# Eight member lists in half the products, search visits placed later, weight loads queued after row stores

## The chip, the cores and the metric

The kernel runs on one core of a Trainium2 chip. The metric is the device time of one execution in microseconds. Before the change three executions took 1294.56 us (median), 1291.51 and 1298.22 us.

## The reference

Three layers follow one another. The first is a retention layer without softmax: for 8 sequences, 8 heads, 576 positions and head size 64, `ret = (q k^T / 8) * D`, with `D[i, j] = gamma_h ** (i - j)` for `j <= i` and 0 elsewhere, and `out = ret v`. This gives `x` of 4608 rows by 512.

The second is a mixture of 8 experts, each row going to one of them:

```
expert_idx = argmax(x_normalised @ emb_normalised.T / tau)
gate       = softmax(logits)[expert_idx]
out[rows]  = gate * (relu(x[rows] @ w1[e]) @ w2[e])     # w1: 512 x 1024, w2: 1024 x 512
```

The third is a mixture of 8 experts of exactly 576 rows each. All 4608 x 8 logits `x @ w_gate` are walked from the largest to the smallest; a row is given to an expert when the row is still free and the expert has fewer than 576 rows. Then `out[rows] = relu(x[rows] @ w1[e]) @ w2[e]`.

## The kernel before, in words

The program has three stages, and the order of each engine's instructions is written out by hand.

Stage A (to about 205 us) computes retention in 36 tiles of 128 rows, routes each row to an expert of the second layer and scatters it to that expert's part of a buffer in HBM.

Stage B (about 215 to 751 us) runs the second layer's experts, five tiles of 128 rows each. Every fp32 operand is split into a high and a low part, and each product is three matrix multiplications (lines 1247 to 1249 for the first product, line 1321 for the second). For `e = 0` the loop over half columns `n` does all first halves and then all second halves; for later experts the halves `h` alternate. Raw weights come in by SyncE's queue into four `raw` buffers (`w_load`, lines 239 and 241). `w_acc` converts one: ScalarE writes the high part (line 267) and its negative (line 248), and GpSimd issues a DMA that adds the raw weight on top (`w_add`, line 251); a `raw` buffer is free again when that DMA is done. The four conversions for the second weight of `e = 0` (`w_conv` at `n` in `CV = (6, 8, 10, 12)`) use a GpSimd subtraction instead (line 272). Each tile's result `yr` (line 1333, two buffers) is stored to HBM by SyncE (line 1335). SyncE works in the order of the program, so a load that waits for its `raw` buffer holds up what stands behind it. In the gaps VectorE makes the third layer's logits by dot products of `yr` with `wgb`, the gate weights broadcast to all partitions (`pull`, line 1171), and those for a small table `M7` (`mpull`, line 1211); every second `yr` goes through TensorE instead (`ytr`, line 1180).

The third layer's assignment is found by eight searches, one after another, each followed by a member list. A search bisects the threshold of the next expert to fill in seven steps. A step has three visits to TensorE: counts (line 875), a fold (line 888) and a spread (line 950), with VectorE work between; three more visits end the search. The member list (`members`) turns the ranks `rk` of 128 x 40 rows into a list of 576 row numbers: four one-hot tiles `ohb` (line 1083), 40 products of 64 stationary and 20 moving columns in two visits (line 1093), the two sums joined (lines 1058 and 1100), a visit in fp32 that puts the halves at their partitions (line 1104), and `idx` (line 1109). Then GpSimd gathers the rows (line 1379).

Stage C (about 751 to 1296 us) runs the third layer's experts (lines 1399 to 1409 for the transposes and splits, 1454 for the first product, 1487 to 1493 for the second). The searches for the later experts run beside the products of the earlier ones. The class `Issue` plans this order: it holds a planned clock for each engine, threads that yield `(engine, duration)`, and places a thread's next step when the planned clocks reach it. A step on TensorE is planned at the end of the thread's previous step plus `HOP["P"]` = 0.25 us, less the thread's `early`. `early` is 0.7 for the first search and its members and 0.0 for the others.

Of the kernel before, what the change touches and what calls it, by code (L numbers as in the profile page):

```python
# [9 lines left out]
F32 = mybir.dt.float32  # L10
F32R = mybir.dt.float32r
BF = mybir.dt.bfloat16
# [145 lines left out]
def moe_kernel(ctx: ExitStack, tc: tile.TileContext, moe_expert_emb, moe_tau, moe_w1, moe_w2,  # L158
# [88 lines left out]
    def w_neg(hi, lo):  # L247
        A.activation(lo, hi.bitcast(F32), AF.Copy, scale=-1.0)  # L248

    def w_add(hi, lo, after=0.0):  # L250
        G.dma_start(lo, RAW[wpos[1]], accum_op=OP.add)  # L251
        w_done_(hi, lo)
        w_load(after=after)

    def w_acc():
        hi, lo = w_high()
# [418 lines left out]
    def search_tables2():  # L675
        for i, sh in enumerate(SHIFTS):
            V.tensor_scalar(jt[i], j0, sh, None, op0=OP.logical_shift_left)
        kj = sc.tile([128, NJ], I32, name="kj")
        V.tensor_tensor(kj, jt[0], kmin.to_broadcast([128, NJ]), op=OP.bitwise_xor)
        V.tensor_scalar(j27, kj, 31, 1, op0=OP.arith_shift_right, op1=OP.logical_shift_right)  # L680
        V.tensor_tensor(j27, j27, kj, op=OP.bitwise_xor)
        for nm in cst:
            SY.dma_start(cst[nm], c[nm])
        V.tensor_copy(descb, desc)
        V.memset(shf, 0.0)
        V.tensor_copy(shf[:, :64], ident[:64, :64])
        V.tensor_copy(shf[:, 192:], ident[:64, :64])
        V.tensor_tensor(lim.rearrange("p (e t) -> p e t", t=T1), rnk[:, None, :].to_broadcast([128, E, T1]),
                        baseL[:, :, None].to_broadcast([128, E, T1]), op=OP.is_lt)
        V.tensor_scalar(lim, lim, -2.0 * NEG, NEG, op0=OP.mult, op1=OP.add)  # L690
        V.memset(rem, float(CAP2))
        V.memset(frz, 0.0)
# [175 lines left out]
    def tl(name, shape, dt=F32, bufs=1):  # L868
        return sw.tile(list(shape), dt, name=name, bufs=bufs)

    def search(p):
# [149 lines left out]
            V.scalar_tensor_tensor(sn[:, z], sn[:, z], r2[:, z:z + 1], mem[:, z], op0=OP.add, op1=OP.mult)  # L1021
        V.scalar_tensor_tensor(rk, sn[:, 0], 1000.0, sn[:, 1], op0=OP.add, op1=OP.add)
        LST.append(p)
        IS.spawn(members(p, rk), p if p < 2 else 3, IS.t["V"], 0.0 if p else 0.7)
        if p < E - 1:
            yield "V", 1.2
            fo = tl("fo", (128, E))
# [11 lines left out]
            V.tensor_tensor(Lw, Lw, eb(acc), op=OP.min)  # L1039

    LST, MDONE, CHT = [], {}, []
    shf = sw.tile([64, 256], F32, name="shf")
    NQ = 4

    RROK = {}

# [8 lines left out]

    def lcopy(p, ls, lq):
        yield "A", 0.2
        A.activation(ls, lq, AF.Copy)
        RROK[p, 1] = IS.t["A"]

    def members(p, rk):
        if p:
            yield lambda: MDONE.get(p - 1)
        yield "V", 0.6
        rki = tl("rki", (128, NSL), I32)
        V.tensor_copy(rki, rk)
        ai = tl("ai", (128, NSL), I32)
        V.tensor_scalar(ai, rki, 6, None, op0=OP.logical_shift_right)
        V.tensor_scalar(rki, rki, 63, None, op0=OP.bitwise_and)
        yield "V", 0.5  # L1070
        ea = tl("ea", (128, NSL, 2 * T2), BF)
        V.tensor_tensor(ea, eb(ai, 2 * T2),
                        a10.rearrange("p r t -> p (r t)")[:, None, :].to_broadcast([128, NSL, 2 * T2]),
                        op=OP.is_equal)
        ohb = []
        ls = tl("ls", (64, 4 * T2))
        rr = tl("rr", (128, NSL, 2, 2, T2), BF)
        IS.spawn(rrows(p, ea, rr), 1, IS.t["V"])
        for z in range(NQ):
            cz = slice(NSL // NQ * z, NSL // NQ * (z + 1))  # L1080
            yield "V", 0.75
            oq = tl(f"ohb{z}", (128, NSL // NQ, 64), BF)
            V.tensor_tensor(oq, rki[:, cz, None].to_broadcast([128, NSL // NQ, 64]),  # L1083
                            i64[:, None, :].to_broadcast([128, NSL // NQ, 64]), op=OP.is_equal)
            ohb.append(oq)
            if z % 2 == 0:
                continue
            if z == 1:
                yield lambda: RROK.get(p)
            yield "P", 1.2, -1.2 if z < NQ - 1 else 0.0  # L1090
            lq = sr()[:64, :4 * T2]
            for cc in range(NSL // NQ * (z - 1), NSL // NQ * (z + 1)):
                P.matmul(lq, ohb[cc * NQ // NSL][:, cc % (NSL // NQ), :],  # L1093
                         rr[:, cc].rearrange("p r z t -> p (r z t)"),
                         start=(cc % (NSL // 2) == 0), stop=((cc + 1) % (NSL // 2) == 0), skip_group_check=True)
            if z == 1:
                IS.spawn(lcopy(p, ls, lq), 1, IS.t["P"])
        yield lambda: RROK.get((p, 1))
        yield "V", 0.25
        V.tensor_tensor(ls, ls, lq, op=OP.add)  # L1100
        yield "P", 0.4
        lp = sr()
        for r in range(2):
            P.matmul(lp[:, :2 * T2], shf[:, 128 * r:128 * r + 128], ls[:, 2 * T2 * r:2 * T2 * r + 2 * T2], start=(r == 0),  # L1104
                     stop=(r == 1), skip_group_check=True)
        yield "V", 0.2
        idx = sw.tile([128, T2], I32, name="idx", bufs=2)
        with nc.allow_low_precision(reason="sums of two whole numbers below 2**24 are exact"):
            V.tensor_reduce(idx, lp[:, :2 * T2].rearrange("p (z t) -> p t z", z=2), axis=AX.X, op=OP.add)
        MDONE[p] = IS.t["V"]  # L1110
        yield lambda: GATHER[0](p)
        yield "G", 1.25 * T2
        XGAT[p] = [IS.t["G"] - 1.25 * (T2 - 1 - t) + 3.2 for t in range(T2)]
        XG2[p] = GATHER[1](idx)
# [3 lines left out]
    def chain():  # L1118
        for p in range(E):
            yield lambda: 0.0  # L1120
            CHT[0][1] = (0, 3, 2)[min(p, 2)]
            CHT[0][5] = 0.0 if p else 0.7
            yield from search(p)

    with tc.tile_pool(name="mb", bufs=1, reuse_waits="tile") as mb, tc.tile_pool(name="mw", bufs=2, reuse_waits="tile") as mw, \
            tc.tile_pool(name="mps", bufs=1, space=PSUM, reuse_waits="tile") as ps:
        wgb = mb.tile([128, E, DM], F32, name="wgb")
        SY.dma_start(wgb.rearrange("p e d -> p (e d)"), ap(c["w_gate_t"], 0, [[0, 128], [1, DM * E]]))
        wgk = mb.tile([128, KD, E], F32, name="wgk")
        SY.dma_start(wgk, moe2_w_gate.rearrange("(k p) e -> p k e", p=128))  # L1130
        s16 = mb.tile([16, E], F32, name="s16")
# [93 lines left out]
        for e in range(E):  # L1225
# [6 lines left out]
            for n in range(2 * KF):  # L1232
# [21 lines left out]
                if n == 3:  # L1254
                    ylg()
                pull()
                if h and (f % 4 or e == 0):
                    mpull()
                if last and n == 2:
                    lg7 = [ps.tile([128, KD, 128], F32, name="tp", bufs=2).rearrange("p k n -> p (k n)")[:2 * E, :m]  # L1260
# [2 lines left out]
                    next(gg, None)  # L1263
                if e == 0 and h:
                    next(gg, None)
                if e and h and f in (0, 1, 3, 5):
                    w_acc()
                if not e and n in CV:
# [42 lines left out]
            for t in range(T1):  # L1311
                if not last:
                    xtr(e + 1, t)
                    for _ in range((1, 2, 1, 0, 0)[t]):
                        w_acc()
                z = slice(128 * t, 128 * t + 128)
                py = ps.tile([128, DM], F32, name="l2", bufs=2)
                for f in range(KF):
                    wh, wl = w2[f]
                    for n, (a, b) in enumerate(((hh, wh), (hh, wl), (hl, wh))):  # L1320
                        P.matmul(py, a[:, f, z], b, start=(f == 0 and n == 0), stop=(f == KF - 1 and n == 2))  # L1321
                        if last:
                            IS.tick(0.234)
                    if f == 1:
                        ytr()
                    if f == 5:
                        ylg()
                    if f % 2:
                        pull()
                yr = mw.tile([128, ROWY], F32, name="yr", bufs=2)  # L1330
                if last:
                    IS.use("A", 0.7)
                A.activation(yr[:, :DM], py, AF.Copy, scale=gts[e][:, t:t + 1])  # L1333
                V.tensor_copy(yr[:, DM:], xe[:, t, :2])
                SY.dma_start(ybuf[e * CAP1 + 128 * t:e * CAP1 + 128 * t + 128, :], yr)
                if not last:
                    if t % 2 == 0:
                        dots.extend((yr, e * T1 + t, j) for j in range(E))
                    else:
                        ytrq.append((yr, e * T1 + t))  # L1340
                    if t % 2:
                        mpull()
                    if t in (1, 3):
                        mpull()

    with tc.tile_pool(name="oc", bufs=2) as oc:
        with tc.If(tv > 0):  # L1347
# [20 lines left out]
    with tc.tile_pool(name="fb", bufs=1, reuse_waits="tile") as fb, tc.tile_pool(name="fw", bufs=2, reuse_waits="tile") as fw, \  # L1368
# [46 lines left out]
        def conv(p, a, b):  # L1415
            for n in range(a, b):
                yield lambda: RAWAT.get(8 * (E + p) + n) if wpos[1] == 8 * (E + p) + n else None
                yield "A", 1.07
                hl = w_high()
                if p == 0 and n < 4:  # L1420
                    yield "V", 1.23
                    w_low(*hl, V)
                    WAT[p, n] = IS.t["V"]
                    continue
                yield "A", 1.07
                w_neg(*hl)
                yield "G", 1.1
                w_add(*hl, 3.0)
                WAT[p, n] = IS.t["G"] + 3.5

        def evac1(p, f, h, pq):
# [141 lines left out]
```

## Time and profile before

| | us |
|---|---|
| median of three executions | 1294.56 |
| the profiled execution's own time | 1298.07 |
| its span, first to last instruction | 1296.3 |
| TensorE matmul busy | 1217.5 (94%) |
| TensorE weight load busy | 1043.9 (81%) |
| VectorE busy | 713.8 (55%) |
| ScalarE busy | 576.9 (45%) |
| GpSimd busy | 328.8 (25%) |
| mean granted TensorE clock (share of 2.4 GHz) | 0.963 |

Busy time counts the time in which at least one instruction of the engine was under way. Matmuls overlap in the pipeline, so the start of one to the start of the next tells what it costs TensorE, not its listed duration. A wait is put down to the instruction that ended it last.

### The profile page before, as it was taken

How to read it: one execution, taken by the hardware profiler on the slowest of the kernel's cores; microseconds unless marked ns; L12 is line 12 of the kernel's file. 1: busy time of each engine (PE TensorE's matmuls, PEld its weight loads, DVE VectorE, ACT ScalarE, POOL GpSimd, SP SyncE). 2: the span in 40 equal slices, each digit the busy share in tenths (PEclk: the TensorE clock that was granted, in tenths of full speed). 3: DMA queues.
4: the chain of work that ended last, by engine and by line, in shares of the span. 5: the costliest groups of instructions: out<-in, count | busy, mean ns of one | idle time of the engine just before them, and what ended most of it. 6: DMA issues, size and time to landing. Idle time of an engine off the chain costs nothing. (4 is left out here: it accounts for less than half of the span.)

```text
span 1296.3 us, 23772 instructions
## 1 busy us (share of the span) xinstructions
PE 1217.5 (94%) x9031; PEld 1043.9 (81%) x9031; DVE 713.8 (55%) x2330; ACT 576.9 (45%) x1090; POOL 328.8 (25%) x451
## 2 busy tenths in 40 slices
PE   6999976799999999999999969999999999899997
PEld 5888865789898989898887658686868878798896
DVE  4566643866565657576565756575857757021120
ACT  3566643345354535453532044353443535274550
POOL 3253454511121313030100021313133231422211
PEclk8999986899999999999999969999999999899999
DMA  7888854566767768686841244757673756677840
GB/s 261 274 282 283 268 212 147 190 164 177 195 177 183 185 168 206 163 213 159 214 127 42 90 127 119 195 137 189 143 183 85 187 152 155 184 172 182 205 100 37
DMA packets 91742, 224.65 MB, mean 173 GB/s; under 512 B 13671, under 2 KB 14447, under 8 KB 91488
## 3 DMA queue, kind: packets, MB, share of 16 engines
q0 software_dynamic: 28272, 90.35, 32.6%
q1 hardware_dynamic: 63344, 132.67, 30.7%
q8 instruction: 73, 1.20, 0.4%
q14 instruction: 53, 0.43, 0.1%
HBM read 130.26 MB, written 40.28 MB: 132 GB/s over the span
## 5 line engine op out<-in xcount | busy, mean ns | idle before, releaser
L1171 DVE SCALAR_TENSOR_TENSOR jk<-yr,wgb 128x512 bf16<-128x512 f32 x168 | 115.4, 687 | 2.4
L1250 ACT ACTIVATE hh<-l 128x320 fp32r<-128x320 f32 x128 | 55.3, 432 | 124.6 <-PE l L1249 112.3
L1333 ACT ACTIVATE yr<-l,gts 128x512 f32<-128x512 f32 x40 | 27.5, 688 | 168.9 <-PE l L1321 65.5
L251 POOL DMA_DIRECT2D w_0l<-raw x29 | 26.7, 920 | 292.2 <-ACT w_0l L248 261.8
L1436 DVE SCALAR_TENSOR_TENSOR h2l<-l,h2h 128x288 fp32r<-128x288 f32 (+2 forms) x128 | 58.3, 456 | 76.9 <-ACT h2h L1434 76.3
L1251 DVE SCALAR_TENSOR_TENSOR hl<-l,hh 128x320 fp32r<-128x320 f32 x128 | 62.4, 487 | 68.7 <-ACT hh L1250 66.2
L1434 ACT ACTIVATE h2h<-l 128x288 fp32r<-128x288 f32 (+2 forms) x128 | 52.3, 409 | 93.2 <-PE l L1454 92.2
L1461 ACT ACTIVATE o<-l 128x512 f32<-128x512 f32 (+1 forms) x40 | 23.7, 593 | 134.1 <-PE l L1493 83.8
L405 DVE TENSOR_TENSOR sm<-s,dt 128x512 f32<-128x512 f32 (+1 forms) x80 | 48.1, 633 | 57.2 <-PE s L402 44.9
L1468 POOL DMA_INDIRECT out_dram<-o,tid x40 | 42.2, 1056 | 137.9 <-ACT o L1461 90.3
L1379 POOL DMA_INDIRECT xg<-ybuf,idx x40 | 42.8, 1069 | 94.5 <-SPq L1347 58.6
L402 PE MATMUL s<-qT,kT 64*128 64x128 f32 x576 | 45.2, 298 | 11.1 <-DMA qT<-qT 8.6
L717 DVE TENSOR_TENSOR xl<-tp,xh 128x512 fp32r<-128x512 f32 (+1 forms) x41 | 27.6, 676 | 50.7 <-ACT xh L716 36.3
L931 DVE TENSOR_TENSOR cmp<-v,kb 128x1280 bf16<-128x1280 f32 (+1 forms) x42 | 54.4, 1295 | 0.2
L1464 DVE TENSOR_TENSOR o<-o,l 64x512 f32<-64x512 f32 x8 | 5.5, 690 | 86.8 <-ACT o L1461 86.8
L1247 PE MATMUL l<-xh,w_0h 128*128 128x320 f32 x128 | 41.4, 323 | 11.9 <-DVE hl L1251 7.6
L402 PEld LDWEIGHTS s<-qT,kT 64*128 64x128 f32 x576 | 38.0, 198 | 17.1 <-issue 9.4
L251 POOL DMA_DIRECT2D w_3l<-raw x29 | 25.3, 874 | 98.5 <-ACT w_3l L248 70.4
L379 POOL TENSOR_TENSOR kd<-kr,gk 128x512 f32<-128x512 f32 (+1 forms) x32 | 34.5, 1080 | 61.8 <-PE st L438 29.3
L251 POOL DMA_DIRECT2D w_2l<-raw x29 | 24.7, 851 | 97.8 <-ACT w_2l L248 61.7
L534 POOL DMA_INDIRECT xs<-xg,r_sli x36 | 37.0, 1027 | 47.0 <-ACT xg L465 26.3
L423 ACT ACTIVATE xT<-o 128x512 f32<-128x512 f32 x36 | 21.5, 597 | 59.9 <-PE o L420 56.8
(374 smaller groups left out, 4131.2 us busy)
## 6 DMA issues: line engine op xcount, KB each, us to landing
raw<-in_moe_w_dram SPq DMA_DIRECT2D x128, 512.0 KB
w_0l<-raw POOLq DMA_DIRECT2D x29, 512.0 KB
w_1l<-raw POOLq DMA_DIRECT2D x29, 512.0 KB
w_2l<-raw POOLq DMA_DIRECT2D x29, 512.0 KB
w_3l<-raw POOLq DMA_DIRECT2D x29, 512.0 KB
ybuf<-yr SPq DMA_DIRECT2D x40, 257.0 KB
xt<-xs SPq DMA_DIRECT2D x39, 261.0 KB
kT<-kT SPq DMA_DIRECT2D x36, 256.0 KB
```

The costliest lines, as they stand in the source:

```text
L251: G.dma_start(lo, RAW[wpos[1]], accum_op=OP.add)
L402: P.matmul(sp[e][:, hp, :], kT[r, hp, :], qT[r, hp, :], start=True, stop=True, skip_group_check=True)
L405: V.tensor_tensor(sm[z, e, :, z], sp[e][z, :, z], dt_t[z, e, :, z], op=OP.mult)
L931: V.tensor_tensor(cmp, bc(v, ALLC, nj), kb.bitcast(F32)[:, None, :].to_broadcast([128, NSL, nj]), op=OP.is_ge)
L1171: V.scalar_tensor_tensor(jk, yr[:, :DM], 1.0, wgb[:, j, :], op0=OP.mult, op1=OP.mult, accum_out=L2V[:, cc, j:j + 1])
L1247: P.matmul(pp, wh[:, fz], xh[:, kk, z], start=(kk == 0), stop=False)
L1250: A.activation(hh[:, f, z], pp, AF.Relu)
L1251: V.scalar_tensor_tensor(hl[:, f, z], pp, 0.0, hh.bitcast(F32)[:, f, z], op0=OP.max, op1=OP.subtract)
L1379: G.indirect_dma_start(out=xg[:m, t, :], out_offset=None, in_=ybuf, in_offset=bass.IndirectOffsetOnAxis(ap=idx[:m, t:t + 1], axis=0))
L1434: A.activation(h2h[:, f, z], pq, AF.Relu)
L1436: V.scalar_tensor_tensor(h2l[:, f, z], pq, 0.0, h2h.bitcast(F32)[:, f, z], op0=OP.max, op1=OP.subtract)
L1468: st = G.indirect_dma_start(out=out, out_offset=bass.IndirectOffsetOnAxis(ap=TID[p][:m, t:t + 1], axis=0), in_=o[:m], in_offset=None)
```

## The change

`early` becomes `LAZY` = -0.35 for the searches and members from the third on, so that their TensorE steps are planned 0.6 us after the operand's planned end. The member list multiplies two 128-row chunks at once: 20 products of 128 stationary and 40 moving columns in one visit, of whose four blocks the two on the diagonal are used; ScalarE copies one and VectorE the other into a bf16 tile `ls` of 128 partitions, and the last visit is in bf16 with `shf` on 128 partitions. In stage B the load that followed each conversion moves: for `e > 0` to every even `n` of the first product, and to the end of each tile of the second, behind the row store. In stage C it stays where it was. The load of `wgb` moves from the start of stage B to `n == 6` of `e = 0`, and the table's dot products in `e = 0` begin at `n = 12` instead of `n = 8`.

```diff
-    def w_add(hi, lo, after=0.0):
+    def w_add(hi, lo):
         G.dma_start(lo, RAW[wpos[1]], accum_op=OP.add)
         w_done_(hi, lo)
-        w_load(after=after)
...
-        V.tensor_copy(shf[:, :64], ident[:64, :64])
-        V.tensor_copy(shf[:, 192:], ident[:64, :64])
+        for z in HALVES:
+            V.tensor_copy(shf[z, :64], ident[z, z])
+            V.tensor_copy(shf[z, 192:], ident[z, z])
...
-        IS.spawn(members(p, rk), p if p < 2 else 3, IS.t["V"], 0.0 if p else 0.7)
+        IS.spawn(members(p, rk), p if p < 2 else 3, IS.t["V"], (0.7, 0.0, LAZY)[min(p, 2)])
...
-    shf = sw.tile([64, 256], F32, name="shf")
-    NQ = 4
+    shf = sw.tile([128, 256], BF, name="shf")
+    NQ, LAZY = 4, -0.35
...
-        A.activation(ls, lq, AF.Copy)
+        A.activation(ls[:64], lq[:64, :4 * T2], AF.Copy)
...
-            if z % 2 == 0:
-                continue
-            if z == 1:
-                yield lambda: RROK.get(p)
-            yield "P", 1.2, -1.2 if z < NQ - 1 else 0.0
-            lq = sr()[:64, :4 * T2]
-            for cc in range(NSL // NQ * (z - 1), NSL // NQ * (z + 1)):
-                P.matmul(lq, ohb[cc * NQ // NSL][:, cc % (NSL // NQ), :],
-                         rr[:, cc].rearrange("p r z t -> p (r z t)"),
-                         start=(cc % (NSL // 2) == 0), stop=((cc + 1) % (NSL // 2) == 0), skip_group_check=True)
-            if z == 1:
-                IS.spawn(lcopy(p, ls, lq), 1, IS.t["P"])
+        yield lambda: RROK.get(p)
+        yield "P", 0.6
+        lq = sr()[:, :8 * T2]
+        for cc in range(0, NSL, 2):
+            c0 = cc % (NSL // NQ)
+            P.matmul(lq, ohb[cc * NQ // NSL][:, c0:c0 + 2, :].rearrange("p c j -> p (c j)"),
+                     rr[:, cc:cc + 2].rearrange("p c r z t -> p (c r z t)"),
+                     start=(cc == 0), stop=(cc == NSL - 2), skip_group_check=True)
+        IS.spawn(lcopy(p, ls, lq), 1, IS.t["P"])
+        yield "V", 0.2
+        V.tensor_copy(ls[64:], lq[64:, 4 * T2:])
         yield lambda: RROK.get((p, 1))
-        yield "V", 0.25
-        V.tensor_tensor(ls, ls, lq, op=OP.add)
...
-            CHT[0][5] = 0.0 if p else 0.7
+            CHT[0][5] = (0.7, 0.0, LAZY)[min(p, 2)]
...
-        SY.dma_start(wgb.rearrange("p e d -> p (e d)"), ap(c["w_gate_t"], 0, [[0, 128], [1, DM * E]]))
...
-                if h and (f % 4 or e == 0):
+                if e == 0 and n == 6:
+                    SY.dma_start(wgb.rearrange("p e d -> p (e d)"), ap(c["w_gate_t"], 0, [[0, 128], [1, DM * E]]))
+                if h and (f % 4 if e else f > 3):
                     mpull()
...
+                if e and not h:
+                    w_load()
                 if e and h and f in (0, 1, 3, 5):
                     w_acc()
...
                     if t in (1, 3):
                         mpull()
+                    w_load()
...
-                w_add(*hl, 3.0)
+                w_add(*hl)
+                w_load(after=3.0)
```

## Rows read from the trace of the kernel before

**Rows 1.** Windows (from:to, length; busy PE, PEld, DVE, ACT, POOL; PEclk, DMA, GB/s).
```profile
771.00:1129.40 358.40, 345.59 (x2532) 280.36 (x2532) 220.04 (x724) 150.21 (x286) 101.72 (x124) 0.97 0.62 158
1129.40:1183.30 53.90, 53.90 (x325) 47.99 (x324) 11.11 (x22) 28.86 (x55) 12.17 (x18) 1.00 0.73 178
```
**Rows 2.** Timeline of PE round two product visits of a member list (start, duration, instruction).
```profile
1103.37 0.40 PE L1493 MATMUL l<-w_2h,h2l 128*128 128x512 f32 x1
1103.70 0.80 PE L1093 MATMUL srb<-rr,ohb 128*64 128x20 bf16 x20
...
1104.77 0.40 PE L1493 MATMUL l<-w_2l,h2h 128*128 128x512 f32 x1
```
**Rows 3.** Timeline of PE round the last visit of a member list.
```profile
1096.94 0.49 PE L1493 MATMUL l<-w_2h,h2l 128*128 128x512 f32 x1
1097.37 0.61 PE L1104 MATMUL srb<-ls,shf 64*128 64x10 f32 x4
...
1098.24 0.40 PE L1493 MATMUL l<-w_2l,h2h 128*128 128x512 f32 x1
```
**Rows 4.** Timeline of PE round a counts visit of a search.
```profile
1054.74 0.39 PE L1489 MATMUL l<-w_1l,h2h 128*64 128x512 f32 x1
1054.97 0.41 PE L875 MATMUL srb<-oh,cmp 128*128 128x32 bf16 x10
...
1055.55 0.39 PE L1489 MATMUL l<-w_2l,h2h 128*64 128x512 f32 x1
```
**Rows 5.** Timeline of PE round the first member list, end of stage B.
```profile
737.50 0.40 PE L1321 MATMUL l<-w_1h,hh 128*128 128x512 f32 x1
...
741.45 0.80 PE L1321 MATMUL l<-w_1h,hl 128*128 128x512 f32 x1
```
**Rows 6.** Windows of 10 us in which the granted clock fell (columns as in rows 1).
```profile
250.00:260.00 10.00, 9.44 (x46) 9.22 (x47) 9.52 (x45) 2.23 (x5) 5.85 (x11) 0.70 0.34 106
740.00:750.00 10.00, 7.63 (x31) 5.35 (x30) 4.82 (x18) 1.63 (x2) 0.00 (x0) 0.66 0.06 23
1040.00:1050.00 10.00, 10.00 (x57) 7.05 (x55) 4.58 (x14) 0.60 (x1) 6.20 (x6) 0.83 0.79 238
1110.00:1120.00 10.00, 9.45 (x31) 7.71 (x32) 0.34 (x2) 0.60 (x1) 4.39 (x7) 0.69 0.74 216
```
**Rows 7.** Waits of PE, 809 to 1130 us (us in total, times, longest).
```profile
PE srb L1104 <- DVE ls L1100: 3.5, 1, 3.5
...
PE srb L875 <- DVE cmp L931: 1.6, 3, 0.9
PE srb L888 <- DVE cs L884: 1.3, 3, 0.6
```
**Rows 8.** Timeline: last split of the third expert's rows, its first product.
```profile
898.38 1.01 DVE L1409 TENSOR_TENSOR xl<-tp,xh 128x512 fp32r<-128x512 f32 x2
...
910.99 0.30 PE L1454 MATMUL l<-xh,w_0h 128*128 128x288 f32 x1
```
**Rows 9.** Waits of PE, 255 to 672 us (stage B from its second expert).
```profile
PE tp L1180 <- ACT yr L1333: 3.6, 6, 1.2
```
**Rows 10.** Timeline of ACT in stage B: a third tile's result.
```profile
341.25 0.69 ACT L1333 ACTIVATE yr<-l,gts 128x512 f32<-128x512 f32 x1 [5.80 <-DMA ybuf<-yr]
```
**Rows 11.** Timeline of SyncE's queue just before it.
```profile
334.96 5.12 SPq L239 DMA_DIRECT2D raw<-in_moe_w_dram  x2
```
**Rows 12.** Waits of PE, 205 to 262 us (the first expert of stage B).
```profile
PE l L1247 <- DVE hl L1251: 5.8, 2, 4.3
```
**Rows 13.** Timeline of DVE, first expert of stage B: a stretched dot product, a late eviction.
```profile
239.44 2.50 DVE L1211 SCALAR_TENSOR_TENSOR jk<-wz,wgb 128x512 bf16<-128x512 f32 x1
...
244.90 2.44 DVE L196 SCALAR_TENSOR_TENSOR g_l<-g_kf,g_l 128x40 f32<-128x40 f32 x1
...
250.02 0.48 DVE L1251 SCALAR_TENSOR_TENSOR hl<-l,hh 128x320 fp32r<-128x320 f32 x1
```
**Rows 14.** Timeline of POOL beside it.
```profile
238.98 2.41 POOL L272 TENSOR_TENSOR w_1l<-raw,w_1h 128x1024 fp32r<-128x1024 f32 x1 [0.27 <-ACT w_1h L267]
```

More of the change, by code (lines that the diff above doesn't have):

```diff
@@ L1075, in members @@
         ohb = []
-        ls = tl("ls", (64, 4 * T2))
+        ls = tl("ls", (128, 4 * T2), BF)
         rr = tl("rr", (128, NSL, 2, 2, T2), BF)
```

## The prediction

> **What bounds the kernel now.** I read the windows by stage first, then TensorE's waits in each stage, then the timeline where a wait or a visit of the search stands. The reader is to see that TensorE sets the end nearly everywhere, and that what can be won is the time in which it does something other than expert products, waits, or runs at its lower clock. The 358.4 us from 771 to 1129 hold the rest of expert 0 and experts 1 to 4 of stage C with the searches beside them; expert 5 alone, with no search, takes 53.9 us [rows 1]. Five such experts would take 270, so the searches cost nearly 90 us in that stretch, all of it on TensorE's path: VectorE is busy 220 us of the 358 and is not the bound. Most of a search's visits do not wait. They cost the switch and their own products, so I price visits by the start of a product before to the start of one after.
>
> **The member list's visits, the largest term.** From 1103.37 to 1104.77 two expert products and one visit of 20 small products pass [rows 2]. The two alone take 2 x 0.234 = 0.47 (the planner's figure for 512 columns, which the undisturbed stretch bears out), so a visit costs 0.93 us, and there are two per list. The last visit costs 1098.24 - 1096.94 - 0.47 = 0.83 [rows 3]. A list thus costs 2 x 0.93 + 0.83 = 2.69. The new visit has 20 products with 128 stationary columns. The nearest row is a counts visit: ten products of 128 by 32 in bf16 cost 0.81 - 0.47 = 0.34 [rows 4], of which the first 0.07 or so is the switch, so ten more cost 0.27 and twenty 0.61; 40 moving columns in place of 32 add about 0.04 to 0.07. I take 0.65. Bounds: 0.61, and 0.93, as an old visit with the same count. The new last visit has two bf16 products where the old one had four fp32 passes: between nothing and the 0.34 of ten products; I take 0.20, the side of few products. A list falls from 2.69 to 0.85, a gain of 1.84 (1.42 to 2.08). Seven lists lie in the stretch from 771 to 1129: 12.9 us (9.9 to 14.6). VectorE and ScalarE have the same number of steps per list as before (an add becomes a copy) and gain or lose nothing.
>
> The first list stands at the end of stage B, where TensorE goes from 737.50 to 741.45 with two products between [rows 5]: 3.95 - 0.47 = 3.48. This one is still planned early (0.7), so a wait for the last one-hot tile and one for the copies stay, about 0.9 together; with 0.85 of work the visit costs 1.75, a gain of 1.7 (0 to 2.6). The list itself isn't late: the gather starts only after the branch at line 1347, when all of stage B is stored. In the window 740 to 750 the granted clock is 0.66 [rows 6], so (1 - 0.66) x 10 = 3.4 us of it are lost to the lower of the two levels, 1.2 GHz, right after this thin stretch. With the thin stretch halved I count half of that: 1.7 (0 to 3.4).
>
> **Slack from the third search on.** From 809 us TensorE waits 1.6 us for a comparison and 1.3 for a fold's operand, and some smaller ones [rows 7]. Placed 0.35 later, two thirds of these should go: 2.0 of 2.9 (0 to 2.9). The window 1040 to 1050 has a clock of 0.83 with TensorE busy all the time [rows 6], 1.7 us lost; there are two such windows, the other at 980 to 990, both right behind two list visits and a fold in close order. With half the list work there I take 2.0 of 3.4 (0 to 3.4).
>
> The longest wait is 3.5 us at 1107, for VectorE's add of the last list [rows 7]; behind it the clock is 0.69 in 1110 to 1120, another 3.1 [rows 6]. The add no longer exists, but what held VectorE I do not see, and a copy may be held the same way: 3.0 of 6.6 (0 to 6.6). This may be an event of the profiled execution, whose 1298.07 lies 3.5 above the median.
>
> The slack's price: a search has 24 TensorE steps, so it ends 24 x 0.35 = 8.4 us later, its list 0.7 more, and this adds up from the third search on. Who waits is the expert whose rows are gathered late. Its tightest place is the third expert: its last split ends at 899.39, its first product starts at 910.99 [rows 8], 11.6 us of room, of which the shift takes 9.1 and TensorE's own gain until then about 5. I charge 1.5 us (-8 to 0). Later experts have more room: the last list has its products at 1103 to 1106 [rows 2], and its expert starts two experts of 53.9 us after 1129.4 [rows 1], at 1237; the 131 us between are more than six delays of 9.1.
>
> **Loads behind row stores.** From the second expert of stage B on, TensorE waits six times, 3.6 us in all, for a result `yr` that ScalarE wrote late [rows 9]. ScalarE waited 5.80 for the row store to free the buffer [rows 10], and the store stood in SyncE's queue behind raw loads that waited for their own buffer, two of them over 5.12 us [rows 11]. After the change the store is issued first. Loads leave up to one tile later (about 6 us), but four buffers are ahead and by the loops each is converted some 20 us or more after it is loaded. The `xt` load also moves ahead of one raw load; the `wz` loads stay behind one. I take 3.4 of 3.6 (-2 to 3.6).
>
> **The start of stage B.** In the first expert TensorE waits 5.8 us in two pieces for `hl` evictions [rows 12]; then 250 to 260 has a clock of 0.70, 3.0 us lost [rows 6]. VectorE is late because single instructions on it are stretched to the end of a GpSimd subtraction: a dot product takes 2.50 us beside GpSimd's 238.98 to 241.39, and a gate step on 40 elements 2.44 beside the next one, and so the eviction comes at 250.02 [rows 13, 14]. Without the four dot products of `n` = 8 to 11, I lay VectorE's list out again: at 239.44 a gate step is stretched instead, the eviction of `n = 9` comes 0.6 earlier, the step that started at 244.90 starts near 243.7, before GpSimd's third subtraction, and the eviction of `n = 10` comes near 245. The third and fourth subtractions then stretch later gate steps, and waits of about 2.8 in smaller pieces stay. Gain 3.0 and 1.3 of the clock: 4.3 (-3 to 8.8). The lower bound is for `wgb`, which now leaves SyncE near 235 in place of 217 and meets other loads: if it lands after about 249, VectorE's first dot product holds back the evictions behind it. The dot products left out here fill gaps of VectorE in the seventh expert.
>
> A rule of the Trainium skill speaks against this term (SBUF — State Buffer, "SBUF: two separate sides"): VectorE and GpSimd share one pair of ports as an exclusive lock, and a VectorE operation with two SBUF inputs, or in a two-port mode, blocks for the whole of a GpSimd operation that reads SBUF. Rows 13 and 14 agree: 2.50 and 2.44 us for instructions that end with GpSimd's. By that rule the lock outlives the dot products, since the gate's steps have SBUF inputs too, and if each subtraction still costs one eviction its whole length, the sum lacks 4.3.
>
> **The sum.** 12.9 + 1.7 + 1.7 + 2.0 + 2.0 + 3.0 - 1.5 + 3.4 + 4.3 = 29.5. The profiled execution took 1298.07 (its span 1296.3 and 1.8 around it), which gives 1268.6. From the median, without the 3.0 for the late add, it is 1294.56 - 26.5 = 1268.1. I predict 1268.5.
>
> **The rivals.**
> Only the products shrink: the visits' waits and the clock's falls stay, or move to other visits, because TensorE reaches a visit earlier than planned (a visit of 0.34 is planned with 0.5). For it: the planner's figures are larger than the rows. Against it: 0.35 of slack is more than most of the waits. The gain is then 12.9 + 1.7 and the stores' 3.4, together 18.0: 1280 from the profiled execution, 1277 from the median; I say 1278.
>
> The lock stays: GpSimd's four subtractions each stretch a gate step and hold an eviction. For it: three gate steps were stretched already. Against it: between them VectorE has 3 us less to do. The start's 4.3 go: 1273.
>
> Nothing to be measured: the first term goes into the place where TensorE waits for gathered rows, because what ends the wait (search, list, gather) is no faster. For it: the gather of an expert can only start when its list is done. Against it: the third expert has 11.6 us of room [rows 8], and later experts have more. The time is within 6 of 1294.56.
>
> Slower: the delayed searches reach the experts. For a loss, experts 2 to 6 would each have to wait for their rows. The price is the delay itself, 9.1 us for each of the five: 45.5, less 29.5, so 1298 + 16 = 1314. It decides where the delay, 9.1 us for the third expert, exceeds its room of 11.6 plus what is still early; only the third is near that.
>
> **How the numbers follow.** Forecast 0.48 (1261 to 1276 alone), only the products 0.18, the lock 0.17, nothing 0.10, slower 0.07. The first three are all faster by over 0.5% (6.5 us, below 1288.1; about what a measurement of this kernel can tell from none): 0.83. Within: 0.10. Slower: 0.07. The range takes in the first three with their bounds: below, all terms near their better end, 1255; above, the lists at 9.9 with the stores alone, 1286.
>
> **What would show it.** Right: 20 products at line 1093's successor in one visit, about 0.65 between neighbours, and four fewer passes in the last visit; the interval between the first products of experts 1 to 5 shorter by near 2 us each; no wait for `yr` in stage B; SyncE's stores at once behind `yr`; an `hl` wait of under 3 us near 245; windows at 740 and 1040 at the full clock. Wrong: a list visit above 0.93; TensorE waiting for the third expert's rows; ScalarE waiting for raw weights in stage B; VectorE waiting for `wgb`.

## The result and the profile after

The changed kernel takes 1274.75 us (median of 4 runs, 1272.62 to 1278.59), the kernel before 1295.41 beside it (4 runs, 1291.51 to 1298.22): ratio 0.9853 [0.9832, 0.9874], faster by 1.5%. The prediction was 1268.5 with a range of 1255 to 1286. The profiled execution of the changed kernel took 1273.87, its span 1272.1, so the spans differ by 24.2 us where the sum had 29.5.

The page of the changed kernel, its head, TensorE's share and the clock in 40 slices:
```profile
span 1272.1 us, 23381 instructions
PE 1197.8 (94%) x8855; PEld 1026.9 (81%) x8855; DVE 716.4 (56%) x2332; ACT 578.7 (45%) x1090; POOL 326.3 (26%) x451
...
PEclk9999986999999999999999979998989999999999
```
TensorE is still the bound at 94%, with 176 instructions fewer: a list had 40 small products and 4 passes and has 20 and 2, and there are eight lists (8 x 22).

Timeline of TensorE round the two visits of one list in the changed kernel (they answer to [rows 2, 3]):
```profile
797.22 0.40 PE L1495 MATMUL l<-w_0h,h2l 128*128 128x512 f32 x1
797.45 0.68 PE L1091 MATMUL srb<-rr,ohb 128*128 128x40 bf16 x20
797.98 0.47 PE L1495 MATMUL l<-w_1h,h2h 128*128 128x512 f32 x1
798.29 0.40 PE L1495 MATMUL l<-w_1l,h2h 128*128 128x512 f32 x1
...
800.39 0.39 PE L1495 MATMUL l<-w_2l,h2h 128*128 128x512 f32 x1
800.62 0.20 PE L1101 MATMUL srb<-ls,shf 128*128 128x10 bf16 x2
800.69 0.47 PE L1495 MATMUL l<-w_2h,h2l 128*128 128x512 f32 x1
801.00 0.39 PE L1495 MATMUL l<-w_3h,h2h 128*128 128x512 f32 x1
```
The product right behind a visit is stretched too (0.31 us to the next start in place of 0.23), so I count as in [rows 2, 3], from the product before a visit to the second product after it, less the two products' 0.47. The product visit costs 798.29 - 797.22 - 0.47 = 0.60 and the last visit 801.00 - 800.39 - 0.47 = 0.14: 0.74 a list where I had 0.85 and the kernel before 2.69.

Windows of the changed kernel: stage C from the first product of expert 0 to that of expert 7, the same less its first 5 us and last two experts, and four stretches of 10 us (from:to, length; busy PE, PEld, DVE, ACT, POOL; PEclk, DMA, GB/s):
```profile
746.40:1213.20 466.80, 450.65 (x3068) 372.53 (x3068) 250.35 (x789) 212.43 (x400) 125.03 (x160) 0.96 0.64 164
751.50:1099.50 348.00, 332.74 (x2319) 268.46 (x2319) 204.09 (x654) 150.54 (x282) 89.17 (x114) 0.96 0.60 155
250.00:260.00 10.00, 10.00 (x54) 8.53 (x53) 8.34 (x45) 5.40 (x8) 4.74 (x7) 1.00 0.39 91
722.00:732.00 10.00, 8.01 (x61) 5.99 (x60) 9.09 (x21) 3.48 (x6) 0.00 (x0) 1.00 0.55 219
880.00:890.00 10.00, 7.01 (x38) 4.46 (x38) 5.33 (x13) 3.28 (x10) 1.54 (x3) 0.59 0.57 188
890.00:900.00 10.00, 10.00 (x64) 9.26 (x63) 4.46 (x14) 5.14 (x10) 0.97 (x1) 0.73 0.07 14
```
The same stretch of the kernel before:
```profile
765.80:1237.30 471.50, 458.66 (x3210) 381.24 (x3209) 246.08 (x777) 210.10 (x398) 126.16 (x160) 0.97 0.65 164
```
The stretch of [rows 1] fell from 358.4 to 348.0, but the searches, delayed by their slack, then reach into expert 5: it takes 59.9 where it took 53.9 with nothing beside it. Over all seven intervals from expert to expert stage C won 471.5 - 466.8 = 4.7 us only. The sum has 18.4 of its 29.5 there.

Waits of TensorE in the changed kernel, 795 to 1100 us (they answer to [rows 7]; us in total, times, longest):
```profile
PE tp L1400 <- DMA xg<-ybuf,idx: 8.3, 6, 2.2
PE srb L875 <- DVE cmp L931: 3.2, 4, 1.2
PE tp L1400 <- PE tp L1400: 1.0, 1, 1.0
PE srb L950 <- DVE fl L947: 1.0, 2, 0.5
```
The 3.5 us for the last list's add are gone, and the wait for gathered rows is first with 8.3 us. It is not new. The same view of the kernel before, 809 to 1130 us, has as its second line, which [rows 7] leaves out:
```profile
PE tp L1399 <- DMA xg<-ybuf,idx: 3.0, 2, 1.8
```
Timeline of the third expert's rows in the changed kernel (VectorE's index, GpSimd's first gather, TensorE's transposes):
```profile
872.04 0.17 DVE L1106 TENSOR_REDUCE idx<-srb 128x5 int32<-128x10 f32 x1
872.49 1.07 POOL L1380 DMA_INDIRECT xg<-ybuf,idx  x1 [1.32 <-DVE idx L1106]
...
880.01 0.66 PE L1400 MATMUL tp<-ident,xg 128*128 128x128 f32 x4 [1.56 <-DMA xg<-ybuf,idx]
881.79 1.09 PE L1400 MATMUL tp<-ident,xg 128*128 128x128 f32 x4 [1.13 <-DMA xg<-ybuf,idx]
```
The first rows are there 7.5 us after the first gather is issued, and TensorE stood at the transpose 1.56 us before that. Round it the clock is 0.59 and 0.73 in two windows, 6.8 us of full speed lost.

Where the 24.2 us between the two profiled executions came from, by first products: stage A, which runs the same code, 2.6; the first expert of stage B 3.8; its next six 4.2; the last with the first list 7.0; the step to stage C 1.8; stage C, unrounded, 4.6; the end 0.1.

To see inside stage C, I took each interval from the start of one expert product or transpose to the start of the next, subtracted the nominal time of the first, and put the rest down to what stood between (work, and in brackets TensorE's idle time). The columns add up to the stretch less 376.8 us of nominal products; the last column is what the granted clock below 1.0 lost, and lies within the others. Where a search visit and transposes of rows stand in one interval, all its idle time is in the search column: 1.8 of the 6.4 before and 2.2 of the 8.6 in the last row are waits in front of transposes.

| kernel, profiled execution | stretch | search visits | list visits | rows | other | clock |
|---|---|---|---|---|---|---|
| before | 471.5 | 39.4 (6.4) | 17.9 (4.8) | 2.2 (1.6) | 22.3 | 13.0 |
| after | 466.8 | 42.5 (5.8) | 5.0 (0.9) | 4.2 (9.5) | 22.1 | 16.5 |
| lists alone | 454.4 | 39.7 (8.3) | 5.8 (2.8) | 2.7 (3.3) | 15.0 | 3.4 |
| slack alone | 469.8 | 38.6 (3.5) | 18.0 (2.0) | 3.0 (7.0) | 20.8 | 11.1 |
| after, no slack | 462.1 | 40.0 (7.9) | 5.8 (2.7) | 2.5 (4.7) | 21.7 | 11.3 |
| after, rows later | 453.8 | 39.9 (8.6) | 5.9 (1.7) | 0.8 (1.0) | 19.1 | 7.9 |

Each row is one execution, not a median: that of "lists alone" is the fastest of its six (1271.71), those of "slack alone" and "after, no slack" are the slowest of theirs (1293.61 and 1274.60).

Stage B is cleaner. From 255 to 655 us the trace of the changed kernel lists no wait of TensorE at all, where [rows 9] has 3.6 us for `yr`. ScalarE's waits in that stretch, changed kernel first, then the kernel before (255 to 672 us):
```profile
ACT yr L1333 <- DMA ybuf<-yr: 18.9, 4, 5.3
```
```profile
ACT yr L1333 <- DMA ybuf<-yr: 58.7, 11, 6.2
```
Four of the eleven waits for the store are left, and they reach no TensorE instruction.

VectorE and GpSimd in the first expert of stage B, changed kernel (they answer to [rows 13, 14]):
```profile
237.30 1.98 DVE L183 TENSOR_SCALAR g_nm<-g_nm 128x5 f32<-128x5 f32 x1
...
242.16 0.48 DVE L1247 SCALAR_TENSOR_TENSOR hl<-l,hh 128x320 fp32r<-128x320 f32 x1
...
242.79 2.44 DVE L202 TENSOR_SCALAR g_p<-g_p 128x40 f32<-128x40 f32 x1
245.26 2.28 DVE L201 TENSOR_TENSOR g_p<-g_p,g_l 128x40 f32<-128x40 f32 x1
...
247.67 0.48 DVE L1247 SCALAR_TENSOR_TENSOR hl<-l,hh 128x320 fp32r<-128x320 f32 x1
```
```profile
236.84 2.41 POOL L271 TENSOR_TENSOR w_1l<-raw,w_1h 128x1024 fp32r<-128x1024 f32 x1 [0.27 <-ACT w_1h L266]
242.79 2.40 POOL L271 TENSOR_TENSOR w_2l<-raw,w_2h 128x1024 fp32r<-128x1024 f32 x1
245.15 2.33 POOL L271 TENSOR_TENSOR w_3l<-raw,w_3h 128x1024 fp32r<-128x1024 f32 x1
```
VectorE in the kernel before, the fourth subtraction's gate step and the eviction of `n = 11`:
```profile
247.83 2.28 DVE L202 TENSOR_SCALAR g_p<-g_p 128x40 f32<-128x40 f32 x1
...
251.81 0.48 DVE L1251 SCALAR_TENSOR_TENSOR hl<-l,hh 128x320 fp32r<-128x320 f32 x1
```
The first product of stage B starts at 214.93 before and at 212.31 after, so times are compared from there. The eviction of `n = 10`, which stood behind both gate steps at 250.02 [rows 13], now comes ahead of them at 242.16: 29.9 us into the stage in place of 35.1. But two gate steps in a row are stretched to 2.44 and 2.28 us, as two were before, and now hold the eviction of `n = 11`: 247.67, 35.4 us in, before 36.9. TensorE still waits 3.8 us for `hl`, 5.8 before [rows 12]. VectorE has no wait for `wgb`.

### The profile page after: what moved, and what is told of

It is laid out like the page before. It is cut to its first block, busy times and chain, and to the rows that moved or that the text cites. A ratio compares the mean times of both kernels' runs of the same rounds, so it can differ in the third digit from the quotient of the medians.

```text
span 1272.1 us, 23381 instructions
## 1 busy us (share of the span) xinstructions
PE 1197.8 (94%) x8855; PEld 1026.9 (81%) x8855; DVE 716.4 (56%) x2332; ACT 578.7 (45%) x1090; POOL 326.3 (26%) x451
## 5 line engine op out<-in xcount | busy, mean ns | idle before, releaser
L1247 DVE SCALAR_TENSOR_TENSOR hl<-l,hh 128x320 fp32r<-128x320 f32 x128 | 62.4, 487 | 66.4 <-ACT hh L1246 60.9
L533 POOL DMA_INDIRECT xs<-xg,r_sli x36 | 36.9, 1024 | 46.8 <-ACT xg L464 26.3
L1408 ACT ACTIVATE xh<-tp 128x512 fp32r<-128x512 f32 (+1 forms) x40 | 22.0, 552 | 58.6 <-PE tp L1400 44.2
```

The costliest lines, as they stand in the source:

```text
L1247: V.scalar_tensor_tensor(hl[:, f, z], pp, 0.0, hh.bitcast(F32)[:, f, z], op0=OP.max, op1=OP.subtract)
```

## The experiments

Each ran in five rounds beside the kernel before. Its median was 1292.0 us beside the first four, 1290.4 beside the next four and 1281.3 beside the last, so only ratios are compared across these groups.

**1. The lists alone**: the changed kernel without its slack and with stage B's loads and `wgb` as before.
```
-    def w_add(hi, lo):
+    def w_add(hi, lo, after=0.0):
...
+        w_load(after=after)
...
-    NQ, LAZY = 4, -0.35
+    NQ, LAZY = 4, 0.0
...
+        SY.dma_start(wgb.rearrange("p e d -> p (e d)"), ap(c["w_gate_t"], 0, [[0, 128], [1, DM * E]]))
...
-                if e and not h:
-                    w_load()
...
```


> The kernel before with the new member list alone (20 products of 128 by 40, bf16 last visit); no slack, loads and wgb as before. First theory: the list gives what its rows say, 2.69 to about 0.9 us per list in eight lists, and nothing takes it back: 12 to 14 us, about 1282. Rival: the shorter list moves the plan of the searches too, and part of the gain goes into waits for gathered rows: 5 to 8 us, about 1288 to 1290.

1275.66 us, ratio 0.9884 [0.9846, 0.9921]: 15.0 below the kernel before by ratio; the interval, 10 to 20, holds the first theory's 12 to 14. The list columns fall from 22.7 to 8.6, and 9.6 less are lost to the clock in the profiled execution.

**2. The slack alone**: the kernel before with the slack.
```
-    NQ = 4
+    NQ, LAZY = 4, -0.35
...
-            CHT[0][5] = 0.0 if p else 0.7
+            CHT[0][5] = (0.7, 0.0, LAZY)[min(p, 2)]
```


> The kernel before with the slack of 0.35 us from the third search on alone. First theory: the lists of the third to fifth expert end after the point from which their transposes are planned, so TensorE waits for gathered rows (6 us more than before) and its clock falls after it (3 us more), while the waits of search visits hardly shrink: 4 to 9 us slower, 1299 to 1304. Rival (the prediction's own): visits wait 2 us less, the clock falls less often, 1.5 us for late rows: 1291 to 1294.

1288.79 us, ratio 0.9966 [0.9946, 0.9987]: faster, so my first theory fell as far as the sign goes; the rival's 1291 to 1294 lay too high as well. The waits of TensorE, 775 to 1235 us, show both sides:
```profile
PE tp L1399 <- DMA xg<-ybuf,idx: 5.2, 5, 1.5
PE tp L1399 <- issue: 1.8, 2, 1.4
PE srb L875 <- DVE cmp L931: 1.6, 2, 1.4
```
The search visits' own waits go from 4.6 (6.4 less 1.8 for rows) to 3.5 and the lists' from 4.8 to 2.0, as the slack is meant to do; the waits in front of transposes go from 3.4 (1.6 and the 1.8) to 7.0.

**3. The change without the slack.**
```
-    NQ, LAZY = 4, -0.35
+    NQ, LAZY = 4, 0.0
```


> The changed kernel with the slack set to 0. First theory: waits for gathered rows fall from 9.6 us to about 4 and the clock falls less: 1265 to 1269, faster than the changed kernel's 1274.75. Rival: the slack was worth something, 1276 to 1279; or neither, 1273 to 1276.

1271.08 us, ratio 0.9829 [0.9792, 0.9866]; with the slack it was 0.9853 [0.9832, 0.9874]. No difference can be told. What the search visits lose, the rows give back: (5.8) and (9.5) become (7.9) and (4.7).

**4. The change with the rows planned later**: the planner takes a gathered tile to be there 6.5 us after the gather in place of 3.2.
```
-        XGAT[p] = [IS.t["G"] - 1.25 * (T2 - 1 - t) + 3.2 for t in range(T2)]
+        XGAT[p] = [IS.t["G"] - 1.25 * (T2 - 1 - t) + (6.5 if p else 3.2) for t in range(T2)]
```


> The changed kernel, slack kept, with the planner's figure for the landing of a gather raised from 3.2 to 6.5 us for all experts but the first, so that TensorE's transposes are placed later. First theory: the waits for gathered rows are a matter of the plan, they fall from 9.6 to under 3 us and the clock with them: 1264 to 1268. Rival: the rows come too late anyway, the wait moves to the first product of the expert: 1273 to 1277.

1267.49 us, ratio 0.98 [0.9764, 0.9835]. Timeline of the third expert's rows (GpSimd's first gather, TensorE's transposes):
```profile
877.01 1.07 POOL L1380 DMA_INDIRECT xg<-ybuf,idx  x1 [2.19 <-DVE idx L1106]
...
886.28 0.60 PE L1400 MATMUL tp<-ident,xg 128*128 128x128 f32 x4
887.08 0.63 PE L1400 MATMUL tp<-ident,xg 128*128 128x128 f32 x4 [0.20 <-issue]
```
The transposes come 9.3 us after the issue and do not wait for rows. From 775 to 1235 us the profile lists no wait for gathered rows, where the changed kernel has 8.3; waits of 3.2 in front of transposes stay, put down to the splits and to nothing that the profile shows. The stretch falls from 466.8 to 453.8.

**5. The loads behind the row stores, alone**: the kernel before with this part.
```
-    def w_add(hi, lo, after=0.0):
+    def w_add(hi, lo):
...
-        w_load(after=after)
...
+                if e and not h:
+                    w_load()
...
+                    w_load()
...
-                w_add(*hl, 3.0)
+                w_add(*hl)
+                w_load(after=3.0)
```


> The kernel before with the weight loads of the second layer's later experts queued behind the row stores, nothing else. First theory: the six waits of 3.6 us in all for yr vanish, the periods of the second to seventh expert fall from 61.5 to 62.5 each to 61.2, and nothing is late for want of weights: 3 to 5 us, about 1288. Rival: a raw load that leaves later makes a conversion wait, no gain: 1292.

1289.73 us, ratio 0.9978 [0.9953, 1.0002], some 2.8 us, with an interval that just reaches no change. From 255 to 672 us TensorE's only listed wait is the first expert's, the six for `yr` are gone:
```profile
PE l L1246 <- DVE hl L1250: 1.9, 1, 1.9
```
The intervals between experts in stage B, from the second to the eighth, are 60.9 to 61.1 where the kernel before has 61.4 to 62.5.

**6. `wgb` and the four dot products, alone.**
```
-        SY.dma_start(wgb.rearrange("p e d -> p (e d)"), ap(c["w_gate_t"], 0, [[0, 128], [1, DM * E]]))
...
-                if h and (f % 4 or e == 0):
+                if e == 0 and n == 6:
+                    SY.dma_start(wgb.rearrange("p e d -> p (e d)"), ap(c["w_gate_t"], 0, [[0, 128], [1, DM * E]]))
+                if h and (f % 4 if e else f > 3):
```


> The kernel before with the gate weights' load at n = 6 and the table's dot products from n = 12 in the first expert, nothing else. First theory: VectorE's list becomes 3 us shorter between the subtractions, but two of GpSimd's four subtractions still stretch gate steps; waits for hl fall from 5.8 to 3.8 us: 2 to 5 us with the clock, about 1288 to 1290, and VectorE doesn't wait for the gate weights. Rival: the late load of the gate weights costs what the dot products give: 1292.

1291.38 us, ratio 1.0007 [0.9985, 1.0029]. The wait is cut as in the changed kernel, the time isn't, by what can be measured. From 205 to 262 us:
```profile
PE l L1246 <- DVE hl L1250: 3.8, 2, 3.2
```

**7. No slack, and the rows later**: the changed kernel with both edits.
```
-    NQ, LAZY = 4, -0.35
+    NQ, LAZY = 4, 0.0
...
+        XGAT[p] = [IS.t["G"] - 1.25 * (T2 - 1 - t) + (6.5 if p else 3.2) for t in range(T2)]
```


> The changed kernel with slack 0 and the planner's figure for the landing of a gather at 6.5 us. If the slack's gain on visits (3 to 4 us of waits) is real and its price lies only in the rows' waits, then with these planned away the slack must show its gain: 1269 to 1272 here, against 1267.5 with slack. Rival: the slack is worth nothing either way: 1266 to 1269.

1267.81 us, ratio 0.9807 [0.9779, 0.9835], beside 0.98 [0.9764, 0.9835] with the slack: with the rows planned later, too, the slack is worth nothing that can be measured.

**8. Experiment 4 without GpSimd's subtractions in the first expert of stage B**: its four conversions go the way of the other experts, by an accumulating DMA.
```
                 if not e and n in CV:
-                    w_conv()
+                    w_acc()
+                    w_load()
```


> The changed kernel with the planner's figure at 6.5 us, and the four conversions of the first expert's second weight by ScalarE's negative and an adding DMA, as for the other experts, in place of GpSimd's subtraction. First theory: the stretched gate steps come from those subtractions, so with none the waits for hl fall from 3.8 us in two pieces to under 1 and no instruction of VectorE takes over 1 us there; 3 to 6 us faster than the same without this edit: 1262 to 1265. Rival: VectorE's list is simply too long beside the first product, and ScalarE has four more passes of 1.05 us: 1267 or more.

1258.02 us (6 runs, 1255.07 to 1259.96), ratio 0.9731 [0.9702, 0.9759]: faster than both kernels. The same gate steps as above, and TensorE's waits from 205 to 262 us:
```profile
237.33 0.16 DVE L183 TENSOR_SCALAR g_nm<-g_nm 128x5 f32<-128x5 f32 x1
...
240.09 0.27 DVE L202 TENSOR_SCALAR g_p<-g_p 128x40 f32<-128x40 f32 x1
240.59 0.19 DVE L201 TENSOR_TENSOR g_p<-g_p,g_l 128x40 f32<-128x40 f32 x1
```
```profile
PE l L1322 <- DMA w_3l<-raw: 1.6, 1, 1.6
```
No gate step is held and no `hl` wait is left; the first expert takes 69.3 us, 74.8 in experiment 4 and 72.4 in the changed kernel. A wait of 1.6 for the accumulated weights is new. The time fell by more than the 3 to 6 us expected: experiment 7, which keeps the subtractions and has no slack, ran beside the same kernel before and took 1266.41 to 1270.73.

**9. The same edit on the kernel before**, where `w_acc` still has its load in `w_add`.
```
-                    w_conv()
+                    w_acc()
```


> The kernel before, with one edit: the first expert's four weight conversions in stage B get their low half as the later experts do (ScalarE writes the negated high half, a DMA accumulates the raw weights onto it) instead of by a subtraction on GpSimd. First theory: the two waits of TensorE for hl evictions, 5.8 us, and the clock's fall behind them, 3.0, come from single VectorE instructions that a GpSimd subtraction holds for up to 2.4 us; without the subtractions the interval from the first expert's first product to the second's goes from 76.3 to 69 or 70, no gate step there is over 1 us long, no hl wait over 0.5 stays, and the time is 6 to 9 us below the kernel before, ratio 0.993 to 0.995, though all other parts of the change are left out. Rival: VectorE is late by its own load in the first expert (evictions, gate steps and twelve dot products), and the four accumulating transfers, 512 KB each, land later than the subtractions ended: the hl waits stay over 3 us, or a wait for the low weights takes their place, and the time is within 2 us of the kernel before.

1277.34 us beside 1281.26, ratio 0.9969 [0.9936, 1.0001]. In the trace the first theory holds: the first expert takes 67.6 us (76.3 before), the `hl` waits are gone, and 250 to 260 has the full clock:
```profile
250.00:260.00 10.00, 10.00 (x50) 8.25 (x51) 6.79 (x23) 7.79 (x10) 2.45 (x3) 1.00 1.03 236
```
The time is 4.0 us lower, less than the 6 to 9 expected, with an interval that just reaches no change. That the subtractions hold VectorE is shown; what the kernel before gains without them is between 0 and 8 us.

## Why the prediction held, and where it did not

**The lists: right.** The column of list work falls from 17.9 to 5.0, the 12.9 of the sum, and experiment 1 has this part, with the first list, alone at 15.0. Counted as the prediction counted it, a list costs 0.74 where I had 0.85. (The column stops at the first product behind a visit and takes in visits at the lower clock; it has 2.56 a list before and 0.71 after.)

**The first list: 2.5 in place of 1.7.** Timeline of TensorE in the changed kernel (it answers to [rows 5]):
```profile
726.85 0.40 PE L1321 MATMUL l<-w_2l,hh 128*128 128x512 f32 x1
...
728.25 0.19 PE L1101 MATMUL srb<-ls,shf 128*128 128x10 bf16 x2 [0.17 <-ACT ls L1058]
728.30 0.47 PE L1321 MATMUL l<-w_3h,hh 128*128 128x512 f32 x1
```
From 726.85 to 728.30 TensorE passes both visits in 1.45 - 0.47 = 0.98, with no wait over 0.2. The window round it, 722 to 732, has the full clock, so the 3.4 us lost behind the list before are gone, and not only the half that I counted.

**The row stores: right.** 4.2 in the six experts of the profiled execution, 2.8 by experiment 5's ratio, 3.4 predicted. The picture was a little too clean: the store still stands behind a raw load in places, and ScalarE waits four times, but TensorE doesn't.

**The start of stage B: mechanism right, size between the forecast and the rival "the lock stays".** As laid out, a gate step (1.98 us) took the stretch of the dot product (2.50), and the eviction of `n = 10` came ahead of the third subtraction. What I missed is what the third and fourth subtractions then hold: two gate steps one behind the other, 4.72 us on VectorE, with the eviction of `n = 11` behind them, and so the second `hl` wait is 3.2 where the text asked for under 3. The wait went down by 2.0, not 3.0. Experiment 6 gives nothing measurable for it, and the clock's 1.3 can't be counted on: the granted clock in 250 to 260 is 1.00 in the profiled execution of the changed kernel and of experiment 7, and 0.72 and 0.67 in experiments 3 and 4, with the same code there and the same two waits. Experiments 8 and 9 take the subtractions away, and with them the waits. The Trainium skill (SBUF — State Buffer, "SBUF: two separate sides") has VectorE and GpSimd share a port pair as an exclusive lock for operations in a two-port mode or with two SBUF inputs; the trace agrees for L201 with two inputs, 2.28 us, to the end of GpSimd's 245.15 + 2.33. L183 and L202, which read one tile, are held as well, 1.98 and 2.44 us; which mode these run in no trace here shows.

**The slack's price: wrong, and this is the step that failed.** I wrote that only the third expert was tight and charged 1.5 us. I measured the room from the last split of an expert's rows to its first product, 11.6 us. That was the wrong end: what the delay meets first is the place at which the planner puts the transposes. It puts those of the first two tiles 3.2 us after the planned end of the second gather's issue, with 1.25 us planned for an issue 5.7 after the first; the rows of the third expert's first tile came 7.5 and those of its second 9.3 us after it (872.49, 880.01, 881.79). The kernel before has the same error, and I passed over its 3.0 us, the waits of the second and the fourth expert. From the fifth on its lists were so early that the transposes came 28 us and more after the gather and the error didn't show. In the changed kernel they come 5.0 to 7.9 us after it for the second to the seventh expert, so the planner's 3.2 decides where they stand, and for the third, fourth and fifth TensorE waits in place for rows still on the way: 8.3 us in place of 3.0, the sign "TensorE waiting for the third expert's rows" among them. To this come 2.0 more of work on the rows, 3.1 more on the search visits (42.5 for 39.4, and 39.9 in experiment 4) and, partly within these, a half-speed clock behind all three places (13.65 us from 881.8 at the lower level, 1.2 GHz), 11.9 of the 16.5 us that the clock loses. Not all of it is the slack's: without slack, in experiment 3, the wait for rows is 4.1, above the 3.0 of the kernel before. Experiment 4 changes the planner's one figure, takes the wait for gathered rows to nothing and the time from a ratio of 0.9853 to 0.98, with intervals that just touch (0.9832 to 0.9874, 0.9764 to 0.9835). I also gave the slack 4.0 us for waits and clock. Its waits did fall when it was alone, and in the changed kernel the search visits wait 5.8 us with it and 7.9 without, but experiments 3 and 7 find no time in it with rows early or late; why the waits it saves don't count is not shown.

**The clock in stage C: wrong sign.** I had 2.0 for the windows near 980 and 1040. These two are at the full clock now, and so is the place of the late add: 6.8 us that were lost there are gone. But behind the waits for rows 11.9 us are lost where it was 3.4, and so the stretch as a whole loses 16.5 us to the lower level where it lost 13.0.

**The late add: right in the profile, cause open.** The wait of 3.5 us is gone. I took it for a possible event of one execution; it is not. In experiment 5 VectorE is idle for over 7 us ahead of the add, and TensorE waits 3.6; in experiment 3, where copies stand in its place, ScalarE is idle ahead of its copy, and TensorE waits 2.7. VectorE's and ScalarE's timelines in the two:
```profile
1097.94 0.17 DVE L1099 TENSOR_TENSOR ls<-ls,srb 64x20 f32<-64x20 f32 x1 [7.78 <-remote]
```
```profile
1098.97 0.18 ACT L1058 ACTIVATE ls<-srb 64x20 bf16<-64x20 f32 x1 [6.92 <-remote]
```
Part of that idle time is before the products that each reads; the last of these starts at 1093.49 in experiment 5 and at 1095.55 in experiment 3. The view names no releaser, but the semaphore that both steps wait for is the one that TensorE raises, and the packed traces have it raised at 1097.84 and 1098.88, 4.4 and 3.3 us after those starts (in the kernel before 4.3), where the other lists of these two executions have 0.2 to 1.1. So TensorE's signal came late, and VectorE and ScalarE were not held by work of their own; why it came late I did not find. In the changed kernel's last list it comes 1.1 us after the product's start: that part of the 3.0 may be a matter of where the list happens to stand, which is not shown.

**The sum.** 29.5 against 24.2, inside the range, but by errors against each other, which is luck: stage C gave 4.6 for the 18.4 that the sum has there, stage B and the step to C 16.8 for 11.1 (the clock lost 19.5 in these two before and 9.3 after, so 10 of the 17 are clock), and stage A, which is the same code, 2.6. Two rivals lie nearer to the 1274.75 than my 1268.5: "the lock stays" with 1273 and "only the products shrink" with 1278. Experiments 1 and 5 give 15.0 and 2.8 of the 19 us that the ratio stands for, close to the 18.0 that the second of these counted, and experiments 3, 6 and 7 find nothing to be measured for the slack or for the start of stage B. The rival "nothing", in which the lists' gain goes into the wait for gathered rows, named the right place and was true in part. "Slower" needed five experts to be late by the whole delay; the wait is 2.2 us and less at a time.

## What to carry to other kernels

When work is delayed in a hand-written or planned order, look for the next place that was planned by an estimate of this work's end, not for the next place that needs its result: an estimate that is too short costs nothing while the work is early (the fifth and later lists of the kernel before) and shows as waits once it is late. Read every line of the waits for that place before pricing a delay: 3.0 us for rows stood there already. Price small visits between large products by start-to-start intervals, and count the old and the new over the same products; this gave the largest term within a tenth. Don't put terms for the clock into a sum from one execution: with the same code and the same wait ahead of it, the granted clock behind was 0.67 in one execution and 1.00 in another.

## What was not expected of the hardware

A list's last visit with two bf16 products of 10 columns costs 0.14 us between expert products, and 20 products of 128 by 40 columns 0.60, beside the 0.83 of the four fp32 passes and the 0.93 of 20 products with half the columns on both sides [rows 2, 3]. A gather's first rows were there 7.5 us after the issue in one place (872.49 to 880.01), and in another, in the kernel before, they were read without a wait 4.5 us after it (942.23 to 946.70). A signal of TensorE's came over 3 us behind its product in three executions. And the kernel before itself took 1281.3 to 1295.4 us, by the median, in the four groups of runs.
